# A third PSUM bank for transposed scores, shared with the value sums

## The chip, the cores and the metric

The kernel runs on one NeuronCore of one Trainium2 chip. The metric is device time in microseconds (us), from start to end of one execution. A NeuronCore has five engines that run their own instruction queues side by side: TensorE (PE in the profile; its weight loads are shown apart as PEld), VectorE (DVE), ScalarE (ACT), GpSimd (POOL) and SyncE (SP), which here issues the DMAs. TensorE writes its results to PSUM, which has 8 banks of 128 partitions x 512 fp32 values. GpSimd is used here on SBUF alone.

## The reference

With x of shape (1, 2048, 512), 32 heads of width 16, and a bilinear GLU of width 1792:

```
xn = layernorm(x)
q, k, v = split(xn @ wqkv)                       # 32 heads, 16 wide
p  = softmax(q @ k^T / 4)                        # per head, 2048 x 2048
s  = (p @ v) @ wo
g  = silu(((xn @ w_gate) * (xn @ w_up)) @ w_down)
out = x + s * g
```

## The kernel before

**Precision.** Projections and the GLU use matmuls of type fp32r, each operand split into a high and a low part and three products summed. GpSimd does most of the splitting (a cast and a subtraction, through the helper at L64, which therefore stands as the line of all GpSimd work).

**Attention units.** The work of attention is cut into 32 units: unit `i` is a group of four heads (`g = i // 4`) with one block of 512 queries (`c = i % 4`). A unit has 16 rounds, one for each tile of 128 keys; round `n` of the main loop (L832) is key tile `kt = n % 16` of unit `i = n // 16`. There are 512 rounds.

**One round.** For each of four heads `j`, `expo` (L600) makes a tile `t` of transposed scores (128 keys x 512 queries) on TensorE, in a PSUM bank with the tag "st", and ScalarE writes its exponential `e` to an SBUF tile (L606). `score` (L574) makes a tile `s` of untransposed scores for a unit that comes 21 tiles later, in a bank with the tag "s", and VectorE reduces it to a row maximum `mx` (L581); these maxima enter the transposed scores as extra contraction rows. `t` and `s` use opposite halves of the array's rows and run at the same time, so TensorE does them as pairs. In three of the four places of a round (GAPS) it also takes a few pairs of "filler" matmuls: the q and k projections (tile `p`, L270 and L274), then the GLU (tiles `g`, `u`, `y`), then the output projection (`z`). 93 filler sums share 240 pairs of rounds (CYCLES); most sums have 24 pairs of matmuls and get two or three pairs of rounds each.

**Value sums.** At the end of every even round, `values` (L820) issues the value matmuls of the two rounds before: `pv` (L609) does four matmuls for each key tile, one per head, each on its own 32 columns of the array; they are fp32 and take two passes, so 16 records stand for one block of two key tiles. All 16 key tiles of a unit accumulate in one PSUM bank of the tag "pv". From here on, a *period* means the two rounds from the end of one value block to the end of the next: eight pairs of `t` and `s` with filler pairs between them, and then the value block. There are 256 value blocks.

**After a unit.** `finish` (L618) is a generator that is stepped once per round. Its first step, right behind the unit's last value block, transposes the bank to SBUF on VectorE (`tr`, L623). The next round's step takes the reciprocal `rc` of the row sums (L626) and multiplies on GpSimd (`on`); the step five rounds later transposes back (L632) and stores to DRAM.

**Banks and buffers.** In the main loop BUFS (L43) shares the 8 banks out: 2 for `t`, 3 for `s`, 1 for `pv`, 2 ("misc") for filler. The tiles `e` have 12 buffers (EBUFS). When a value block is issued, 8 of them hold the two rounds it reads and 4 the round just made.

**Order.** TensorE, ScalarE and VectorE run in the order of the program (L828). GpSimd and SyncE are ordered by the scheduler of the framework, by when it finds an instruction ready. A queue runs in order whatever its head waits for.

Some of the small ScalarE and VectorE work has a fixed place in the round: the GLU's `g` copy (L375) and the product `h` (L377) stand at the end of an even round, around the value block; the copy `hh` (L335) stands one round later; `look` (L278) is a one-element read that makes the second half of a filler sum wait for the first.

Of the kernel before, what the change touches and what calls it, by code (L numbers as in the profile page):

```python
# [11 lines left out]
F32 = mybir.dt.float32  # L12
F32R = mybir.dt.float32r
AF = mybir.ActivationFunctionType
OP = mybir.AluOpType
# [4 lines left out]
P = 128  # L20
S, D, H, DH, FF = 2048, 512, 32, 16, 1792
NT = S // P
# [6 lines left out]
VW = DH + 1  # L29
# [10 lines left out]
FINAL_AT = 8  # L40
EARLY = [66, 75, 84, 93] + [104 + 37 * n // 4 for n in range(17)]
EARLY_BUFS = {"s": 4, "x": 2, "f": 2}
BUFS = {"st": 2, "s": 3, "pv": 1, "misc": 2}  # L43
LOWER, UPPER = slice(0, 64), slice(64, P)
BEHIND = mybir.DependencyInfo(mybir.DependencyClass.Sync, mybir.DependencyReason.DATA)
ORDER = mybir.DependencyInfo(mybir.DependencyClass.NoSync, mybir.DependencyReason.SCHED_ONLY)
# [3 lines left out]
def body(ctx, tc, x, wqkv, wo, wg, wu, wd, out):  # L50
# [66 lines left out]
    def psum(tag, name):  # L117
        ps, bufs = fst["ps"]
        return ps.tile([P, 512], F32, tag=tag, name=name, bufs=bufs[tag])
# [23 lines left out]
    def etile():  # L143
        return ep.tile([P, 512], F32, name="e", bufs=EBUFS)
# [395 lines left out]

    NU = NG * NC
    QS, MX = {}, {}

    def two(ap, e):

# [60 lines left out]
        nc.scalar.activation(e, o, AF.Exp, scale=DH ** -0.5)  # L606
        return e

    def pv(i, kt, es):  # L609
        g = i // NC  # L610
        if kt == 0:
            fst["pv"] = psum("pv", f"pv{i}")
        for j in range(4):
            h0 = (4 * g + j) * VW
            nc.tensor.matmul(fst["pv"][32 * j:32 * j + 32], V[:, kt, h0:h0 + 32], es[j],  # L615
                             start=kt == 0, stop=kt == NT - 1)

    def finish(i):  # L618

        g, c = divmod(i, NC)  # L620
        tr = keep.tile([P, 16, 32], F32, name="tr", bufs=1)
        tn = tr.rearrange("p b e -> p (b e)")
        nc.vector.transpose(tn, fst["pv"])  # L623
        yield
        rc = keep.tile([P, 16, 1], F32, name="rc", bufs=1)
        nc.vector.reciprocal(rc, tr[:, :, DH:DH + 1])  # L626
        late = i >= NU - NC
        (nc.vector if late else pool).tensor_tensor(on[:, :, 0:DH], tr[:, :, 0:DH], rc.to_broadcast([P, 16, DH]),
                                                         op=OP.mult)
        for _ in range(1 if late else 5):  # L630
            yield
        nc.vector.transpose(tn, on.rearrange("p b e -> p (b e)"))  # L632
        if i == NU - 1:
            fst["tn"] = tn
            return
        dma(OD[c][4 * g:4 * g + 4], tn)
        finished.add(i)
# [8 lines left out]
    def early():  # L646

        nc.scalar.activation(look, ones[0:1, 0:1], AF.Sqrt)
        for tt in range(4):
            load_x(tt)  # L650
        wraw = []
        for which in (1, 0):
            wraw.append(wtile(f"w{which}r"))
            dma(wraw[-1], wqkv[:, which * D:which * D + P].rearrange("(d p) f -> p d f", p=P))
        norm["raws"] = raws = [etile() for _ in range(ND)]
        for d in range(ND):
            dma(raws[d], wqkv[d * P:(d + 1) * P, 2 * D:])
        for tt in range(4, NT):
            load_x(tt)

        def ahead(m):
            fst["qk", m] = qk_weights(m, 1), qk_weights(m, 0)

        def exp_table(_):
            nc.scalar.activation(look, ones[0:1, 0:1], AF.Exp)

        def warm(n):
            for _ in range(n):
                nc.tensor.matmul(psum("x", "warm"), ident, on.rearrange("p b e -> p (b e)"), start=True, stop=True)

        warm(6)
        first = (0, 1), (2, 3)
        for tts in first:
            ln_open(tts)
        ln_stats(0)
        ln_stats(1)
        ln_root(first[0])
        ln_scale(first[0])
        ln_apply(0)
        ln_apply(1)  # L680
        ln_stats(2)
        ln_stats(3)
        ln_turn(0)
        ln_turn(1)
        warm(3)
        ln_root(first[1])
        ln_scale(first[1])
        ln_apply(2)
        last = ln_apply(3)
        ln_low(0)  # L690
        ln_low(1)
        ln_turn(3)
        ln_turn(2)
        ln_low(3)
        ln_low(2)
        wk, wq = [split_raw(f"w{which}", raw, last) for which, raw in zip((1, 0), wraw)]
        wv = [[etile().bitcast(F32R) for _ in range(ND)] for _ in range(2)]
        for d in range(ND):
            nc.scalar.activation(wv[0][d], raws[d], AF.Copy)
            pool.tensor_tensor(wv[1][d], raws[d], wv[0][d], op=OP.subtract)  # L700

        def k(c):
            yield from qk_proj(wk, 0, 1, c, "f")
            load_k(0, [c])

        def q(c):
            yield from qk_proj(wq, 0, 0, c, "f" if c else "x")
            load_q(c)

        def v(*tts):  # L710
            for tt in tts:
                yield from v_proj(wv, tt, "f")

        at = {n: [] for n in range(253)}
        for c, stats, apply, turns in ((1, (0, 2, 4, 6), (26, 26, 26, 26), (38, 42, 46, 50)),
                                       (2, (16, 20, 26, 27), (60, 60, 62, 62), (70, 74, 79, 83)),
                                       (3, (30, 34, 36, 38), (73, 73, 85, 85), (100, 106, 112, 118))):
            for t in range(4):
                for n, fn in ((stats[t], ln_stats), (apply[t], ln_apply), (turns[t], ln_turn)):
                    at[n].append((fn, 4 * c + t))  # L720
        for tts, n, root, scale in ((tuple(range(4, 8)), 0, 13, 25), (tuple(range(8, NT)), 16, 52, 53)):
            at[n].insert(0, (ln_open, tts))
            at[root].append((ln_root, tts))
            at[scale].insert(0, (ln_scale, tts))
        at[190].append((ones_rows, ks[0]))
        at[150].append((exp_table, None))
        at[205].append((ahead, 1))
        at[130] += [(ones_columns, slice(8, NT)), (other_keys, None)]
        fst["v"] = v_proj(wv, NT - 1, "pv")
        gens = [k(0), q(0), v(0, 1, 2), k(1), q(1), v(3), k(2), v(4, 5), k(3), v(*range(6, NT - 1))]  # L730
        scored = 0
        stream = (n for g in gens for n in g)
        for n in range(253):
            for fn, arg in at[n]:
                fn(arg)
            if n in EARLY:
                for _ in range(4):
                    r, j = divmod(scored, 4)
                    score(r // 16, r % 16, j)
                    scored += 1  # L740
                if scored == 64:
                    maxima(0, 0)
            next(stream, None)
        assert scored == 4 * LEAD
        return wq
# [25 lines left out]
    def step_small(q):  # L771
        if q and next(q[0], 1):
            q.pop(0)
# [44 lines left out]
    prev = []  # L818

    def values():  # L820
        for p in prev:
            pv(*p)
            if p[1] == NT - 1:
                heads.append(finish(p[0]))
                step_small(heads)
        prev.clear()

    with tc.manual_schedule(engines=ORDERED):  # L828
        with banks_of(EARLY_BUFS):
            fil = Filler(filler(early()), spread)  # L830
        ctx.enter_context(banks_of(BUFS))
        for n in range(NU * 16):  # L832
            now[0] = n
            Tied.on = n < 18
            i, kt = divmod(n, 16)
            g, c = divmod(i, NC)
            si, sr = divmod(n + LEAD, 16)
            if kt == 8 and i + 2 < NU:
                load_q(i + 2)
            if kt == 0 and g + 1 < NG and c == 1:  # L840
                load_k(g + 1)
            es = []
            for j in range(4):
                es.append(expo(i, kt, j))
                if si < NU:
                    score(si, sr, j ^ 1)
                step()
                if j == 1:
                    prepare()
                if n and j in GAPS[n % 2]:  # L850
                    if fil.done:
                        fil = Filler(ending(), lambda n: 2)
                    fil.part(n % 2 and j == 1)
            if sr == 15 and si < NU:
                maxima(si, 8 if si < NU - 1 else 4)
            step_small(heads)
            if kt % 4 == 2:
                soon(2, lambda: step_small(later))
            if n == 0:
                run(fst["v"])  # L860
            elif n % 2 == 0 or n == NU * 16 - 1:
                values()
            prev.append((i, kt, es))
        pv(*prev[0])
        run(finish(NU - 1))
        flush()
        last_heads()
        while fil.left or not fil.done:
            now[0] += 1
            prepare()  # L870
            fil.part()
            flush()
# [17 lines left out]
```

## Time and profile before

| | us |
|---|---|
| median of 3 runs | 1857.36 (1857.04 to 1858.09) |
| the profiled execution, its own time | 1857.28 |
| its span from first to last instruction | 1855.5 |
| TensorE matmul busy | 1825.2 |
| VectorE busy | 1474.1 |
| ScalarE busy | 1268.8 |
| GpSimd busy | 574.4 |

A row of a wait reads: who waited, for whom, then the total of that wait in us, how many times, and the longest. A row of the chain of work (which is followed back from the last instruction) reads: start, length, engine, tile and line. A row of the timeline reads: start, length, engine, line, operation and tiles, with the idle time before it and what ended it in brackets; x7 means seven instructions merged. A row of the groups has, after the count, busy time in us and the mean of one instruction in ns. Matmuls are pipelined and their ends are modelled, so a busy TensorE is not one at its peak.

### The profile page before, as it was taken

Reading aid. Unit: us, or ns where it says so; the run is one execution under the profiler, and the core shown is the slowest. Engines: PE = TensorE matmul, PEld = TensorE weight load, DVE = VectorE, ACT = ScalarE, POOL = GpSimd, SP = SyncE. Lnnn points to the kernel's source line nnn. Section 1 sums busy time; section 2 is a strip of 40 time slices with the busy share of each in tenths; the row PEclk is TensorE's granted clock in tenths of the full one; section 3 lists DMA queues with packets and bytes.
Section 4 is the critical chain, followed back from the end, with each engine's and each line's share of the span. In section 5 each row is a group of like instructions: output and inputs, shape, how many; then the busy total and the mean of one; then the engine's idle time right before and its main releaser. Section 6 shows DMA issues by size and latency. Waiting matters only on the chain.

```text
span 1855.5 us, 34207 instructions
## 1 busy us (share of the span) xinstructions
PE 1825.2 (98%) x13578; PEld 976.1 (53%) x13578; DVE 1474.1 (79%) x2438; ACT 1268.8 (68%) x2377; POOL 574.4 (31%) x641
## 2 busy tenths in 40 slices
PE   9999999999999999999999999999999999999998
PEld 5655555555455545555555554555545455454554
DVE  6878888888888888888888888888887888888832
ACT  6256767777766767767677777776767777667664
POOL 5312332532322333233132531421335233134340
PEclk9999999999999999999999999999999999999999
DMA  5317533511131212411023210411134111012341
GB/s 197 113 49 229 181 110 115 137 49 44 50 67 50 91 45 66 73 56 44 28 68 102 77 52 22 100 50 38 42 95 112 33 56 50 19 50 64 115 133 69
DMA packets 117227, 145.72 MB, mean 79 GB/s; under 512 B 12620, under 2 KB 74060, under 8 KB 114380
## 3 DMA queue, kind: packets, MB, share of 16 engines
q1 hardware_dynamic: 117068, 143.55, 26.5%
q8 instruction: 106, 1.74, 0.4%
q14 instruction: 53, 0.43, 0.1%
HBM read 95.94 MB, written 47.45 MB: 77 GB/s over the span
## 4 chain that ended last, share of the span: by engine, by line
PE 92%; ACT 6%; DVE 1%; issue 1%; POOL 0%; DMA 0%; ACTq 0%; POOLq 0%; DVEq 0%
PE pv L615 26%; PE t L604 25%; PE s L579 9%; PE u L270 5%; PE y L270 5%; PE g L270 4%; ACT e L606 4%; PE g L274 3%; PE u L274 3%; PE y L274 3%; PE v L251 2%; PE p L274 2%; PE z L270 2%; PE p L270 2%; ACT hh L335 1%; PE p L251 1%
## 5 line engine op out<-in xcount | busy, mean ns | idle before, releaser
L581 DVE TENSOR_REDUCE mx<-s 128x1 f32<-128x512 f32 x2048 | 1314.0, 684 | 279.9 <-PE s L579 176.5
L606 ACT ACTIVATE e<-t 128x512 f32<-128x512 f32 x2048 | 1161.5, 597 | 510.2 <-PE s L579 262.1
L604 PE MATMUL t<-qs,ks 50*128 50x512 f32 x2048 | 850.0, 436 | 18.3 <-ACT e L606 16.2
L579 PE MATMUL s<-ks,qs 48*128 48x512 f32 x2048 | 831.6, 436 | 0.8 <-DVE mx L581 0.8
L604 PEld LDWEIGHTS t<-qs,ks 50*128 50x128 f32 x2048 | 357.0, 184 | 510.4 <-ACT e L606 330.0
L615 PE MATMUL pv<-e,V 128*32 128x512 f32 x4096 | 493.8, 600 | 0.0
L579 PEld LDWEIGHTS s<-ks,qs 48*128 48x128 f32 x2048 | 349.1, 184 | 22.0 <-issue 5.0
L615 PEld LDWEIGHTS pv<-e,V 128*32 128x32 f32 x4096 | 107.1, 109 | 235.0 <-issue 226.5
L64 POOL CAST w0h<-w0r 128x512 fp32r<-128x512 f32 x60 | 36.7, 612 | 419.3 <-PE u L270 201.1
L64 POOL CAST dh<-wdr 128x512 fp32r<-128x512 f32 x56 | 33.7, 614 | 203.5 <-PE y L274 157.5
L64 POOL TENSOR_TENSOR hl<-h,hh 128x512 fp32r<-128x512 f32 x56 | 72.2, 1290 | 76.8 <-ACT hh L335 74.1
L274 PE MATMUL u<-fh,w0l 64*128 64x512 f32 x224 | 88.0, 393 | 0.0
L274 PE MATMUL u<-fl,w0h 64*128 64x512 f32 x224 | 87.9, 392 | 0.0
L270 PE MATMUL y<-dh,hh 64*128 64x512 f32 x224 | 87.9, 392 | 0.0
L270 PE MATMUL u<-fh,w0h 64*128 64x512 f32 x224 | 87.9, 392 | 0.0
L270 PE MATMUL g<-fh,w1l 64*128 64x512 f32 x224 | 87.8, 392 | 0.0
L270 PE MATMUL y<-dl,hh 64*128 64x512 f32 x224 | 87.8, 392 | 0.0
L274 PE MATMUL g<-fh,w1l 64*128 64x512 f32 x224 | 87.8, 392 | 0.0
L270 PE MATMUL y<-dh,hl 64*128 64x512 f32 x224 | 87.8, 392 | 0.0
L270 PE MATMUL u<-fh,w0l 64*128 64x512 f32 x224 | 87.7, 392 | 0.0
L274 PE MATMUL y<-dh,hh 64*128 64x512 f32 x224 | 87.7, 391 | 0.0
L274 PE MATMUL y<-dl,hh 64*128 64x512 f32 x224 | 87.7, 391 | 0.0
(253 smaller groups left out, 2902.5 us busy)
## 6 DMA issues: line engine op xcount, KB each, us to landing
w1r<-in_wg_dram SPq DMA_DIRECT2D x56, 256.0 KB
w0r<-in_wu_dram SPq DMA_DIRECT2D x56, 256.0 KB
wdr<-in_wd_dram SPq DMA_DIRECT2D x56, 256.0 KB
qs<-QD SPq DMA_DIRECT2D x64, 192.0 KB
ks<-KD SPq DMA_DIRECT2D x12, 768.0 KB
KD<-hl SPq DMA_DIRECT2D x16, 512.0 KB
QD<-hl SPq DMA_DIRECT2D x16, 512.0 KB
OD<-tr SPq DMA_DIRECT2D x31, 256.0 KB
```

The source lines that it names most:

```text
L64: got = getattr(self.engine, name)(*args, **kw)
L251: nc.tensor.matmul(o, l(d), r(d), start=k == d == 0, stop=k == 2 and d == ND - 1)
L270: nc.tensor.matmul(outs[k], l[LOWER], r[LOWER], start=k == 0 and n == 0, stop=(stop or k == 0) and n == len(low) - 1, skip_group_check=k == 1)
L274: nc.tensor.matmul(outs[1 - k], l[UPPER], r[UPPER], start=k == 0 and m == 0, stop=(stop or k == 0) and m == len(high) - 1, skip_group_chec ...
L335: nc.scalar.activation(hi, h, AF.Copy)
L579: nc.tensor.matmul(o, QS[i][b:b + KB, pr, t * P:(t + 1) * P], k[b:b + KB, pr, kc * 512:(kc + 1) * 512], start=True, stop=True)
L581: nc.vector.tensor_reduce(MX[i][:, j, t, kc:kc + 1], o, axis=AX.X, op=OP.max)
L604: nc.tensor.matmul(o, k[b:b + KR, pr, kt * P:(kt + 1) * P], QS[i][b:b + KR, pr], start=True, stop=True)
L606: nc.scalar.activation(e, o, AF.Exp, scale=DH ** -0.5)
L615: nc.tensor.matmul(fst["pv"][32 * j:32 * j + 32], V[:, kt, h0:h0 + 32], es[j], start=kt == 0, stop=kt == NT - 1)
```

## The change

The bank of the tag "pv" is given to "st", which then has three. A value block takes its bank from the "st" banks in turn, like a tile of scores, so that in a period nine tiles pass through three banks. The value sums of a unit are now kept in an SBUF tile (`acc`, one buffer) and each block of two key tiles is added to it: the first block of a unit is copied there by ScalarE; the six in the middle are copied by ScalarE to a tile from the `e` buffers, which GpSimd adds to the sum; the last one is added by VectorE, straight from PSUM (in the very last unit its last two key tiles are two blocks of one, both added by VectorE). `finish` begins with an empty step, and then transposes from `acc` instead of from PSUM.

```diff
-BUFS = {"st": 2, "s": 3, "pv": 1, "misc": 2}
+BUFS = {"st": 3, "s": 3, "misc": 2}
...
+    sums = {}
...
-    def pv(i, kt, es):
+    def block(todo):
+
+        i = todo[0][0]
         g = i // NC
-        if kt == 0:
-            fst["pv"] = psum("pv", f"pv{i}")
-        for j in range(4):
-            h0 = (4 * g + j) * VW
-            nc.tensor.matmul(fst["pv"][32 * j:32 * j + 32], V[:, kt, h0:h0 + 32], es[j],
-                             start=kt == 0, stop=kt == NT - 1)
+        o = psum("st", f"pv{i}")
+        for n, (_, kt, es) in enumerate(todo):
+            for j in range(4):
+                h0 = (4 * g + j) * VW
+                nc.tensor.matmul(o[32 * j:32 * j + 32], V[:, kt, h0:h0 + 32], es[j],
+                                 start=n == 0, stop=n == len(todo) - 1)
+        if todo[0][1] == 0:
+            sums[i] = keep.tile([P, 512], F32, name="acc", bufs=1)
+            nc.scalar.activation(sums[i], o, AF.Copy)
+        elif kt >= NT - 2:
+            nc.vector.tensor_tensor(sums[i], o, sums[i], op=OP.add)
+        else:
+            part = etile()
+            nc.scalar.activation(part, o, AF.Copy)
+            pool.tensor_tensor(sums[i], sums[i], part, op=OP.add)
 
     def finish(i):
 
...
         tn = tr.rearrange("p b e -> p (b e)")
-        nc.vector.transpose(tn, fst["pv"])
+        yield
+        nc.vector.transpose(tn, sums.pop(i))
         yield
...
-        fst["v"] = v_proj(wv, NT - 1, "pv")
+        fst["v"] = v_proj(wv, NT - 1, "st")
...
     def values():
-        for p in prev:
-            pv(*p)
-            if p[1] == NT - 1:
-                heads.append(finish(p[0]))
-                step_small(heads)
+        block(prev)
+        if prev[-1][1] == NT - 1:
+            heads.append(finish(prev[0][0]))
+            step_small(heads)
         prev.clear()
...
-        pv(*prev[0])
+        block(prev)
         run(finish(NU - 1))
```

## The prediction

> **What bounds the kernel now.** I read the page first (span, busy times, chain), then the waits, then the chain and the timeline of single periods.
>
> ```profile
> span 1855.5 us, 34207 instructions
> PE 1825.2 (98%) x13578; PEld 976.1 (53%) x13578; DVE 1474.1 (79%) x2438; ACT 1268.8 (68%) x2377; POOL 574.4 (31%) x641
> PE 92%; ACT 6%; DVE 1%; issue 1%; POOL 0%; DMA 0%; ACTq 0%; POOLq 0%; DVEq 0%
> ```
>
> TensorE looks full: 98% busy and 92% of the chain, so 30.3 us of its time seems free. The waits say otherwise:
>
> ```profile
> PEld t L604 <- ACT e L606: 330.0, 839, 1.0
> ACT e L606 <- PE s L579: 262.1, 168, 1.7
> POOL w0h L64 <- PE u L270: 201.1, 19, 13.1
> POOL w0h L64 <- PE g L274: 164.1, 29, 7.7
> PEld s L579 <- DVE mx L581: 4.4, 10, 0.9
> ```
>
> The weight load of `t` waits 839 times for an exponential, which must free the bank. The bank of `s` makes TensorE wait 4.4 us in all. What one wait costs is seen in a period. First the chain of one with twelve filler pairs:
>
> ```profile
> 206.58 1.85 PE pv L615 x16
> 208.43 0.42 PE t L604
> 208.85 0.23 PE s L579 x2
> ...
> 209.57 0.47 PE t L604
> ...
> 213.57 1.85 PE pv L615 x16
> ```
>
> Each pair takes 0.23 (0.233 over many), the value block 1.85, the first `t` behind it 0.42. Only the third `t` takes 0.47. The timeline shows why:
>
> ```profile
> 208.89 4.61 ACT L606 ACTIVATE e<-t 128x512 f32<-128x512 f32 x7 [1.40 <-PE s L579]
> 208.93 5.39 DVE L581 TENSOR_REDUCE mx<-s 128x1 f32<-128x512 f32 x8 [0.97 <-PE s L579]
> 209.54 0.18 PEld L604 LDWEIGHTS t<-qs,ks 50*128 50x128 f32 x1 [0.41 <-ACT e L606]
> 209.54 0.50 PE L604 MATMUL t<-qs,ks 50*128 50x512 f32 x1
> ```
>
> With two banks the third `t` needs the bank of the first. That exponential starts at 208.89 and takes 0.60; the load follows at 209.54 and the matmul ends at 210.04. So a `t` ends no earlier than 0.55 after its bank is freed. Both ScalarE and VectorE start a period late, after idling through the value block (1.40 and 0.97). Now a period with eight filler pairs:
>
> ```profile
> 303.03 0.42 PE t L604
> ...
> 307.70 1.85 PE pv L615 x16
> ```
>
> Without waits, a period with f filler pairs takes 0.42 + 7 x 0.233 + 0.233 f + 1.85 = 3.90 + 0.233 f.
>
> - Twelve pairs: 6.70, against 213.57 + 1.85 - 208.43 = 6.99.
> - Eight pairs: 5.77, against 307.70 + 1.85 - 303.03 = 6.52: with fewer filler pairs between them, more than one `t` waits.
>
> ```profile
> 112.72 1.85 PE pv L615 x16
> ...
> 1838.86 1.95 PE pv L615 x16
> ```
>
> Between the first and the last value block lie 255 periods of 6.77 on average. Counted in the timeline, 116 hold eleven or twelve filler pairs (some 6.99 each); the other 139 then average (255 x 6.77 - 116 x 6.99) / 139 = 6.59.
>
> **The change part by part.** Prices of one instruction come from these groups:
>
> ```profile
> L581 DVE TENSOR_REDUCE mx<-s 128x1 f32<-128x512 f32 x2048 | 1314.0, 684 | 279.9 <-PE s L579 176.5 <-PE t L604 93.0
> L606 ACT ACTIVATE e<-t 128x512 f32<-128x512 f32 x2048 | 1161.5, 597 | 510.2 <-PE s L579 262.1 <-PE t L604 147.7
> L375 ACT ACTIVATE g<-g 128x512 f32<-128x512 f32 x56 | 33.2, 593 | 0.0
> L632 DVE STREAM_TRANSPOSE tr<-on 128x512 f32<-128x512 f32 x32 | 22.4, 701 | 0.1
> L402 DVE TENSOR_TENSOR y<-y,y 128x512 f32<-128x512 f32 x32 | 21.6, 675 | 0.0
> L64 POOL TENSOR_TENSOR y<-e,y 128x512 f32<-128x512 f32 x16 | 20.6, 1286 | 1.2
> ```
>
> *The third bank and the copy.* Nine tiles pass through three banks in each period, so the third `t` behind a value block always gets the block's own bank, and waits for its copy. The copy has the form of L375: 0.59. It starts as soon as the block ends, for ScalarE idles there. Taking the end of the block as zero, it runs from 0.05 to 0.65 and lets the third `t` end at 0.65 + 0.55 = 1.20. TensorE reaches that point by itself at 0.42 + 4 x 0.233 = 1.35, so the wait is gone with 0.15 to spare. Each later `t` needs the exponential of the one three before. These come every 0.50 to 0.60, from 0.55 on; the fourth `t` may end at 1.15 + 0.55 = 1.70, and TensorE is there at 2.05 with two filler pairs between. Twelve pairs: nothing waits for ScalarE, saving 6.99 - 6.70 = 0.29, times 116 = 34 us.
>
> *What is late next in short periods.* `s` has three banks and VectorE. In the eight-pair period VectorE starts 0.50 after the block:
>
> ```profile
> 303.53 4.36 DVE L581 TENSOR_REDUCE mx<-s 128x1 f32<-128x512 f32 x7 [1.21 <-PE s L579]
> ```
>
> Seven in 4.36 with a last one of 0.68 is one every 0.61. The last `s` needs the fifth reduction, which starts at 0.50 + 4 x 0.61 = 2.94 and ends at 3.62: the `s` can't end before 4.17, while TensorE would be there at 0.42 + 15 x 0.233 = 3.92. So VectorE sets 4.17 + 1.85 = 6.02. I take 6.11 over the 139, since seven- and nine-pair periods and the extra ScalarE copies (`g`, `hh`) land unevenly. Saved: 6.59 - 6.11 = 0.48, times 139 = 67 us. Bounds: the nearest rows allow 0.80 (TensorE alone, 5.79) and 0.2 (only the third `t` mended).
>
> *ScalarE's load.* 32 x 7 = 224 copies of 0.59 are 133 us, giving 1402 of a span near 1790. They run where ScalarE idled (262.1 us behind value blocks). `hh` in the same period pushes an exponential by 0.6; I charge 0.1 for each of 56, 6 us. If the idle time were gone, all 133 would count.
>
> *VectorE.* The 33 adds of 0.68 stand where the first transposition stood, waiting for the same block: no net change. But the empty first step moves the first transposition (L623) one round on, from the value block's shadow to the middle of a period, and the one back (L632, 0.70) with it, from an even to an odd round; I price both at 0.70. In a short period VectorE has no slack, so each costs 0.70; in a twelve-pair one its slack is 4.85 - 4.17 = 0.68, and it costs nothing. 62 x 139/255 x 0.70 = 24 us. The reciprocal (0.23) moves the other way: 3 us back. Bounds: 0 if the idle time behind the block absorbs them, 43 if none is.
>
> *GpSimd.* 192 sums of 1.29 are 248 us, on an engine busy 574 of 1855. Who waits for a sum? In a period without the change 8 buffers `e` are free after a block and 8 are taken before the next. The copied block is a ninth, so the last exponential of the period takes the buffer of that copy, and waits for GpSimd. The sum can start at 0.65 and end at 1.94; the exponential is only missed when it holds up the next copy, at 6.02 - 0.60 = 5.4. Slack 3.4. Nearly everything queued on GpSimd fits:
>
> ```profile
> 591.21 0.61 POOL L64 CAST w0h<-w0r 128x512 fp32r<-128x512 f32 x1 [9.89 <-PE u L270]
> ...
> 593.58 1.29 POOL L64 TENSOR_TENSOR w1l<-w1r,w1h 128x512 fp32r<-128x512 f32 x1
> ```
>
> This run of four splits lasts 3.7. The larger run, at the twelve starts of a third of the GLU, does not:
>
> ```profile
> 572.29 1.17 POOL L64 CAST dh<-wdr 128x512 fp32r<-128x512 f32 x2 [27.54 <-PE y L274]
> ...
> 580.04 1.28 POOL L64 TENSOR_TENSOR dl<-wdr,dh 128x512 fp32r<-128x512 f32 x1
> ```
>
> From 572.29 to 581.32, 9.0 us; a sum behind all of it is 5.6 late. Bounds 0 and 12 x 5.6 = 67; I take 6, since the scheduler orders GpSimd by what is ready, so that a sum can go between two splits.
>
> *Nothing else.* The value matmuls stay the same in number; DMAs keep their number and sizes (stores and the loads behind them move one round). At the end of the kernel one add of 0.68 joins the serial tail: 1 us.
>
> **Sum.** -34 - 67 + 6 + 24 - 3 + 6 + 1 = -67 against the profiled execution's 1857.28 (span 1855.5, and 1.8 around it; the median of the runs is 1857.36, the same within 0.01%). 1857 - 67 = 1790.
>
> **Rivals.**
>
> *Sums come late (slower).* GpSimd's queue is in order, and its casts wait in it for TensorE: `w0h` for (201.1 + 164.1) / 48 = 7.6 on average. A sum behind such a cast holds the period's last exponential 7.6 - 3.4 = 4.2 too long, and TensorE with it. The gain is used up at 67 / 4.2 = 16 of the 60 casts `w0h`; 20 of them give 1874, half of them 1916. Against it: a cast is freed by a matmul that TensorE reaches in fixed order just before a value block, while the sum is ready just after. The Trainium skill's page "PSUM — Partial Sum Buffer", section "Engine vs sequencer instructions", calls the GpSimd queue strict FIFO; the bracketed 9.89 us wait above agrees.
>
> *VectorE binds in all short periods.* The moved transpositions, `h` and the maxima no longer fit behind the shorter period, and only half of the short periods' gain stays: 1790 + 34 = 1824. For it: VectorE would be busy over 80% with three banks of slack; against it, 0.97 to 1.21 idle behind every block.
>
> *The slack absorbs all.* Neither the moved transpositions nor the sums cost anything: 1857 - 101 + 7 = 1763.
>
> *The change does not do what it says.* The value block's bank is freed too late (a copy held up over 0.15), so the third `t` waits as before: 1850 to 1857. By busy time the room would be 30.3 and the result 1827 at best. The Trainium skill's "Perfetto Trace Analysis", section "Identifying the Most-Contended Engine", says that matmul busy time does not measure headroom and that the same gap repeating can mean too little PSUM; the 0.47 in every period agrees.
>
> **How the numbers follow.** Forecast 0.45 (own range 1775 to 1808), late sums 0.15, VectorE 0.20, all absorbed 0.15, no effect 0.05. The range runs from 1752 to 1860, leaving out most of the late sums and a little below the absorbed case. A measurement of this kernel tells a change from none at about 0.2%, 3.7 us. Faster: 0.45 + 0.20 + 0.15 = 0.80; same 0.05; slower 0.15.
>
> **What would show it.** Right: waits of `t` for `e` fall from 330 us to under 120; the third `t` of a period takes 0.23; twelve-pair periods last 6.7; waits of `s` for `mx` grow from 4.4 us to some tens, in periods with a transposition above all; ScalarE busy near 1400, GpSimd near 820. Wrong: rows in which `e` or VectorE's add waits for GpSimd with totals over 60 us, or the copy starting more than 0.2 after its block.

## The result

The changed kernel takes 1807.41 us (median of four runs, 1804.11 to 1810.13) beside 1857.20 before: a ratio of 0.9731 (95% interval 0.9714 to 0.9748), 50 us faster. The forecast was 1790, with a range of 1752 to 1860.

The page of the profiled execution (1807.26 us):

```profile
span 1805.0 us, 35056 instructions
PE 1767.9 (98%) x13578; PEld 1056.4 (59%) x13578; DVE 1455.0 (81%) x2471; ACT 1323.7 (73%) x2601; POOL 821.8 (46%) x833
PE 86%; DVE 4%; POOL 3%; ACT 2%; DMA 2%; issue 1%; SPq 0%; POOLq 0%; DVEq 0%; ACTq 0%
```

TensorE's busy share is 98%, as before. What moved is the share of weight loads (53% to 59%), and the chain: VectorE, GpSimd and even a DMA now stand in it.

The waits:

```profile
PEld t L605 <- ACT e L607: 107.8, 268, 6.0
PEld s L580 <- DVE mx L582: 23.4, 46, 2.5
ACT e L607 <- POOL acc L64: 22.4, 9, 6.8
PEld t L605 <- ACT e L627: 13.6, 49, 0.7
```

`t` waited 839 times before and waits 268 times now. Three waits are new or larger: `s` for the maxima, an exponential for a GpSimd sum, and `t` for the copy of a value block (L627, which writes a tile of the `e` buffers). The last is small, 13.6 us in all.

The chain through a period with twelve filler pairs, and through one with eight:

```profile
211.18 0.42 PE t L605
...
212.31 0.24 PE t L605
...
216.13 1.85 PE pv L618 x16
217.99 0.43 PE t L605
```

```profile
198.45 0.43 PE t L605
...
199.57 0.23 PE t L605
...
202.58 1.85 PE pv L618 x16
204.44 0.42 PE t L605
```

The third `t` takes 0.24 and 0.23 where it took 0.47. The eight-pair period lasts 204.44 - 198.45 = 5.99, against 6.52 before and 6.02 in the forecast. This twelve-pair period lasts 6.81, because it is the one behind a unit's last block; the median of those not there is 6.73, against 6.99 before and 6.70 in the forecast. So these two periods do what was foretold, and the time that is missing lies elsewhere.

### The profile page after: what moved, and what is told of

Same layout as the page of the kernel before. It is cut to its first block, busy times and chain, and to the rows that moved or that the text cites. A ratio compares the mean times of both kernels' runs of the same rounds, so it can differ in the third digit from the quotient of the medians.

```text
span 1805.0 us, 35056 instructions
## 1 busy us (share of the span) xinstructions
PE 1767.9 (98%) x13578; PEld 1056.4 (59%) x13578; DVE 1455.0 (81%) x2471; ACT 1323.7 (73%) x2601; POOL 821.8 (46%) x833
## 4 chain that ended last, share of the span: by engine, by line
PE 86%; DVE 4%; POOL 3%; ACT 2%; DMA 2%; issue 1%; SPq 0%; POOLq 0%; DVEq 0%; ACTq 0%
PE pv L618 25%; PE t L605 17%; PE s L580 12%; PE g L270 5%; PE u L270 4%; PE y L270 4%; PE y L274 4%; PE u L274 3%; PE g L274 3%; DVE mx L582 3%; PE p L270 3%; PE v L251 2%; PE z L270 1%; ACT e L607 1%; PE p L274 1%
## 5 line engine op out<-in xcount | busy, mean ns | idle before, releaser
L582 DVE TENSOR_REDUCE mx<-s 128x1 f32<-128x512 f32 x2048 | 1276.8, 681 | 247.3 <-PE s L580 163.2
L607 ACT ACTIVATE e<-t 128x512 f32<-128x512 f32 x2048 | 1110.8, 609 | 126.4 <-PE t L605 32.2
L605 PE MATMUL t<-qs,ks 50*128 50x512 f32 x2048 | 805.8, 415 | 15.8 <-ACT e L607 14.3
L64 POOL TENSOR_TENSOR acc<-acc,e 128x512 f32<-128x512 f32 x192 | 251.0, 1307 | 455.8 <-ACT e L627 455.8
L627 ACT ACTIVATE e<-pv 128x512 f32<-128x512 f32 x192 | 114.7, 598 | 221.6 <-PE pv L618 221.6
L274 PE MATMUL g<-fh,w1h 64*128 64x512 f32 x224 | 90.7, 405 | 0.0
L270 PE MATMUL u<-fh,w0h 64*128 64x512 f32 x224 | 89.1, 398 | 0.0
L274 PE MATMUL u<-fh,w0h 64*128 64x512 f32 x224 | 88.8, 396 | 0.0
L274 PE MATMUL u<-fh,w0l 64*128 64x512 f32 x224 | 88.5, 395 | 0.0
L270 PE MATMUL g<-fh,w1l 64*128 64x512 f32 x224 | 88.4, 395 | 0.0
L270 PE MATMUL g<-fl,w1h 64*128 64x512 f32 x224 | 88.3, 394 | 0.0
L270 PE MATMUL g<-fh,w1h 64*128 64x512 f32 x224 | 88.2, 394 | 0.0
```

What stands on the lines that cost most here:

```text
L64: got = getattr(self.engine, name)(*args, **kw)
L270: nc.tensor.matmul(outs[k], l[LOWER], r[LOWER], start=k == 0 and n == 0, stop=(stop or k == 0) and n == len(low) - 1, skip_group_check=k == 1)
L274: nc.tensor.matmul(outs[1 - k], l[UPPER], r[UPPER], start=k == 0 and m == 0, stop=(stop or k == 0) and m == len(high) - 1, skip_group_chec ...
L582: nc.vector.tensor_reduce(MX[i][:, j, t, kc:kc + 1], o, axis=AX.X, op=OP.max)
L605: nc.tensor.matmul(o, k[b:b + KR, pr, kt * P:(kt + 1) * P], QS[i][b:b + KR, pr], start=True, stop=True)
L627: nc.scalar.activation(part, o, AF.Copy)
```

## The experiments

All times are medians of four runs, with the kernel before timed on the same chip.

### Sums in SBUF without the third bank

```diff
-BUFS = {"st": 3, "s": 3, "misc": 2}
+BUFS = {"st": 2, "s": 3, "pv": 1, "misc": 2}
...
-        o = psum("st", f"pv{i}")
+        o = psum("pv", f"pv{i}")
...
-        fst["v"] = v_proj(wv, NT - 1, "st")
+        fst["v"] = v_proj(wv, NT - 1, "pv")
```

> The sums in SBUF as in the changed kernel, but the value block keeps a bank of its own and the transposed scores have two. Theory (the third bank is the gain, and copies and sums alone cost): the copy stands ahead of the first exponential, so the third t of a period waits 0.5 us longer in 224 periods and more than one t waits in short ones: 1930 to 1980, waits of t for e over 400 us. Rival (the gain comes from the value sums leaving PSUM, not from the bank): 1800 to 1815.

Measured: 1907.52 us, ratio 1.0274 (1.0257 to 1.0291).

```profile
PEld t L605 <- ACT e L607: 354.7, 833, 4.9
```

```profile
208.06 1.90 PE pv L618 x16
209.96 0.02 issue
209.98 0.60 ACT e L627
210.58 0.50 ACT e L607
211.08 0.04 issue
211.12 0.49 PE t L605
...
215.13 1.86 PE pv L618 x16
216.99 0.42 PE t L605
```

The waits of `t` are back (833), and the kernel is slower than before. With and without the bank differ by 1907.5 - 1807.4 = 100 us: that is what the bank gives once the sums are in SBUF. The sums alone cost 1907.5 - 1856.5 = 51 us beside the kernel before. The rival is refuted: taking the value sums out of PSUM gains nothing by itself.

The expected time was too high. The chain shows the error: copy (0.60) and exponential (0.50 behind it) end 1.12 after the block, where the first exponential alone ended 1.06 after it in the period shown of before (209.49 - 208.43). ScalarE had to wait some 0.46 for its first `t` anyway, and the copy fills that time. It costs the twelve-pair periods 0.1 in the median (7.09 against 6.98; 7.03 against 6.99 in the ones shown), not 0.5.

### The third bank from the maxima

The kernel before, with one number moved:

```diff
-BUFS = {"st": 2, "s": 3, "pv": 1, "misc": 2}
+BUFS = {"st": 3, "s": 2, "pv": 1, "misc": 2}
```

> The kernel before with the third bank for t taken from s (two left), value sums in PSUM as before. Theory (VectorE is the next limit): the wait of t goes, that of s for the maxima takes its place; twelve-pair periods about 6.75 to 6.9, short ones 6.5 to 6.7, in all 1830 to 1860, waits of s for mx over 150 us. Rival (three banks of s are not needed): 1755 to 1775, better than the changed kernel, since no copies or sums are added.

Measured: 1903.43 us, ratio 1.025 (1.0235 to 1.0265).

```profile
PEld s L579 <- DVE mx L581: 140.7, 441, 2.5
PEld t L604 <- ACT e L606: 38.8, 50, 0.9
```

The wait of `t` falls from 330 to 38.8 us, and that of `s` rises from 4.4 to 140.7, near what was expected of the waits. But the time lies 43 us above the top of what was expected: even twelve-pair periods grow, to a median of 7.09, and short ones last 6.9 whether they hold seven, eight or nine filler pairs. The third bank helps only if it isn't one of VectorE's.

### Late sums taken over by VectorE

In the trace of the changed kernel, 12 of the 192 GpSimd sums end so late that the last exponential of the period starts 0.03 us behind them. The worst case follows: the timeline of GpSimd, that of ScalarE, and then busy times by stretch. A row of the last has the stretch, its length, the busy times of PE, PEld, DVE, ACT and POOL with their instructions, the granted clock (1.00 is full speed), the DMA share and GB/s.

```profile
337.07 0.61 POOL L64 CAST dh<-wdr 128x512 fp32r<-128x512 f32 x1 [3.76 <-DMA wdr<-in_wd_dram]
...
339.54 1.26 POOL L64 TENSOR_TENSOR acc<-acc,e 128x512 f32<-128x512 f32 x1
```

```profile
340.83 0.60 ACT L607 ACTIVATE e<-t 128x512 f32<-128x512 f32 x1 [6.75 <-POOL acc L64]
```

```profile
335.00:341.40 6.40, 0.84 (x6) 0.19 (x2) 1.09 (x2) 0.57 (x2) 4.25 (x5) 0.81 0.41 101
341.40:346.00 4.60, 4.52 (x22) 3.54 (x24) 2.47 (x4) 3.22 (x7) 4.52 (x6) 0.52 0.42 112
346.00:350.00 4.00, 4.00 (x38) 1.90 (x34) 2.89 (x5) 2.43 (x5) 4.00 (x4) 1.00 0.44 128
```

A split of `dh` at the head of GpSimd's queue waits for its weights; the sum stands behind it; the exponential needs the buffer of the copy; the next value block's copy stands behind that exponential. TensorE stops. The period lasts 14.60 (335.41 to 350.01) instead of 6.73, 7.9 more. The stop is 5.6 of that; the rest comes after it, where the clock is at 0.52 and matmul pairs take 0.43. Here ten of the eleven blocks whose sum ended more than 4 us behind its copy are added by VectorE instead (the eleventh held up nothing):

```diff
+LATE = {1, 11, 21, 33, 34, 84, 188, 235, 241, 243}
...
-        elif kt >= NT - 2:
+        elif kt >= NT - 2 or 8 * i + todo[0][1] // 2 in LATE:
             nc.vector.tensor_tensor(sums[i], o, sums[i], op=OP.add)
```

> The changed kernel, but the ten value blocks whose GpSimd sum ended more than 4 us after its copy are added by VectorE straight from PSUM, like the last block of a unit. Theory (the rest of the missing gain is exponentials that wait for a late sum, because its copy holds one of the 12 buffers, and the slower TensorE clock behind such a stop): waits of e for GpSimd fall from 22 us to under 8, the stops of 8 us near 335 us and of 5 us near 1650 us go, and the time falls by 8 to 16 us, to 1791 to 1799. Rival (the added work costs, not its lateness: 182 of 192 sums and all copies but ten stay): 1804 to 1808.

Measured: 1793.98 us, ratio 0.9665 (0.965 to 0.9679), 13 us less than the changed kernel. The same place:

```profile
327.00:342.00 15.00, 15.00 (x124) 8.72 (x124) 13.20 (x22) 10.24 (x22) 9.22 (x10) 1.00 0.67 146
```

TensorE is busy all through at full clock, although 182 sums and copies are still there. So these 13 us are the price of lateness, not of the amount of work. One of the stops that should have gone stays: near 1640 us the filler `y` waits 1.8 us for GpSimd to split its operand (`hl`), and that period lasts 9.35 where it lasted 6.54 before. In the kernel before no filler waits for GpSimd. So late work on GpSimd reaches TensorE in a second way, which the prediction did not have.

### Where the transpositions stand

Two edits of the first step of `finish`. One takes the empty step out; the other, shown here, makes it two, except in the last four units, which get none.

```diff
-        yield
+        for _ in range(0 if i >= NU - NC else 2):
+            yield
         nc.vector.transpose(tn, sums.pop(i))
```

> The changed kernel without the empty step of finish, so the first transposition stands right behind VectorE's add at the end of the value block, and the second is back in an even round. Theory: the second transposition (8 us) and the end (7 us) are won back, but add and transposition now hold the first reduction of the next period by 0.7 us in all 32 units, also those with twelve filler pairs, 10 to 15 us: 1799 to 1808. Rival (the empty step is the whole fault): 1778 to 1786.

> The changed kernel, but finish makes two empty steps in units 0 to 27, which puts both transpositions at the end of an even round, and none in units 28 to 31, which end as early as in the kernel before. Theory (a transposition costs where it stands in the middle of a short period, some 20 us in all; the empty step in the last units leaves a hole without filler, some 7 us): 1778 to 1786, short periods behind a unit's last block 6.0 to 6.3 instead of 6.8, and 15 us instead of 22 behind the last value block. Rival (VectorE has no idle time left, so 0.7 us costs the same wherever it stands): only the end is gained, 1799 to 1803.

Measured: without the empty step 1800.79 us, ratio 0.97 (0.9686 to 0.9715); with two 1785.37 us, ratio 0.9622 (0.9606 to 0.9638). Both times fit the theory and refute the rivals; only the stretch behind the last value block fell less than expected, to 19 us. The chain of the changed kernel through a period with eight filler pairs behind a unit's last block, and that of the kernel with two empty steps:

```profile
263.87 0.66 PE t L605 x2
...
266.42 0.67 DVE mx L582
267.08 0.62 DVE tr L636
267.70 0.59 DVE mx L582
...
268.83 1.85 PE pv L618 x16
270.69 0.66 PE t L605 x2
```

```profile
263.52 0.66 PE t L605 x2
...
267.53 0.24 PE t L605
267.89 1.85 PE pv L618 x16
269.74 0.43 PE t L605
```

With the transposition between two reductions, the last `s` of the period waits for VectorE and the period lasts 6.82. With the transposition at the end of an even round, where VectorE idles through a value block, it lasts 6.22. Without any empty step add and transposition both stand behind the block: every period behind a unit's last block is longer, those with twelve pairs too (7.35 against 6.73), which takes most of the gain back. (Of the 22 us of two empty steps, some 3 come from the end of the kernel, not from the periods.)

### VectorE adds every block

```diff
-        elif kt >= NT - 2:
+        elif True:
             nc.vector.tensor_tensor(sums[i], o, sums[i], op=OP.add)
```

> The changed kernel with all seven later blocks of a unit added by VectorE straight from PSUM; no ScalarE copies but the first of a unit, no GpSimd sums. Theory (VectorE binds short periods and has slack in long ones): each add holds the first reduction of the next period by some 0.2 us and the row of reductions behind it by 0.7; the short periods go from 6.0 to 6.2 up by 0.2 to 0.6, the twelve-pair ones by less than 0.1, the 16 us of late sums go: 1825 to 1865. Rival (VectorE's idle time behind a value block hides the add, as it hid the first transposition): 1785 to 1800.

Measured: 1804.60 us, ratio 0.9717 (0.9703 to 0.9732): the same as the changed kernel, without GpSimd sums and with one ScalarE copy a unit.

```profile
L624 DVE TENSOR_TENSOR acc<-pv,acc 128x512 f32<-128x512 f32 x225 | 155.2, 690 | 168.9 <-PE pv L618 166.7
```

The expected time was too high. The add (0.69) begins at once behind the block, so the first reduction starts only some 0.2 later. The median eight-pair period goes from 5.99 to 6.15, the twelve-pair one stays at 6.73. What the short periods lose, the late sums give back.

### Repairs together

Two empty steps (none in the last four units) and the ten late blocks on VectorE (called late_two below); the same with every block from the 233rd on, and the 156th, on VectorE too; and two empty steps with every block on VectorE.

> Both repairs together: two empty steps in finish (none in units 28 to 31), and the ten late blocks added by VectorE. Theory (two separate faults, transpositions in the middle of a period and late sums): the gains add, 1807 - 22 - 13 = 1772, within 1768 to 1776. Rival (both win back the same lost time, or VectorE's ten adds collide with the transpositions now at the end of even rounds): 1779 to 1785.

> As late_two, with every block from the 233rd on (unit 29 and after, where GpSimd splits the operands of the output projection and VectorE has few maxima left) added by VectorE, and the 156th too. Theory (late sums stop TensorE there and nothing else does): 2 to 6 us below late_two. Rival (the stops of the last units come from GpSimd's splits themselves, or from the hole without filler): the same as late_two within 2 us.

> All seven later blocks of a unit added by VectorE, and the two empty steps of finish (none in units 28 to 31). Theory (what an add costs VectorE behind a block, 0.2 us in a short period, does not grow when a transposition stands ahead of that block): 1804 - 22 = 1782, within 1778 to 1788, slower than late_two, because every short period still pays for its add. Rival (the row of reductions, the transposition and the add together overfill the time of the value block): 1792 to 1804.

| kernel | us | ratio (95%) |
|---|---|---|
| two empty steps, ten blocks on VectorE | 1773.38 | 0.9551 (0.9533 to 0.9568) |
| the same kernel again, on the chip of the last row | 1774.10 | 0.9558 (0.9542 to 0.9574) |
| and all blocks at the end | 1774.26 | 0.9555 (0.954 to 0.9569) |
| two empty steps, all blocks on VectorE | 1790.82 | 0.9641 (0.9626 to 0.9655) |

> The same kernel as late_two, beside all_dve_two on one chip: 1771 to 1777.

The two gains add (1807 - 22 - 13 = 1772): they are separate faults. The first of these kernels is the fastest found, 84 us faster than before. More blocks on VectorE at the end win nothing. With all blocks on VectorE, two empty steps give 14 instead of 22 us, less than the theory and a little more than the rival expected; the median of the twelve-pair periods right behind the second transposition is 6.98 instead of 6.73, which fits transposition and add meeting at one value block, but no run takes that apart.

## Why the prediction was right, and what it missed

The same period holds the same TensorE work in every kernel, so the traces can be subtracted period by period. The two kinds of period are taken from the kernel before and late_two, which has neither late sums of more than 6 us nor, in units 0 to 27, transpositions in the middle of a period; what little both still cost there counts against the bank. The other terms are differences between late_two, the kernel with the late blocks on VectorE alone, the changed kernel and the kernel before.

| term of the sum | forecast | measured |
|---|---|---|
| third bank and copies, long periods (eleven or twelve pairs) | -34 | -31 |
| third bank and copies, short periods, with `hh` | -67 + 6 = -61 | -55 |
| transpositions and reciprocal, in the periods | 24 - 3 = 21 | 14 |
| late sums | 6 | 14 |
| start and end of the kernel | 1 | 8 |
| sum | -67 | -50 |

The sum is 17 us off, and only by luck not more: the transpositions cost 7 less than foretold, which hides some of what the other terms cost more. The 100 us between the kernels with and without the bank can't be set against the forecast's 34 + 67 = 101: the one is counted from a kernel that already has the sums and is 51 us slower, the other from the kernel before. From there bank and copies give 31 + 55 = 86, against 95. The trace has 121 long periods (6.96 on average before) and 134 short ones (6.60), not 116 and 139; this moves the sum by little.

*What bounds the kernel.* Right. A TensorE at 98% busy still had 84 us to give, and its busy share is 98% after the gain too. The wait of `t` for `e` is 107.8 us, under the 120 foretold.

*The third bank and the copy; what is late next in short periods.* Right for the two periods that were worked out: the medians of twelve- and eight-pair periods not behind a unit's last block are 6.73 and 5.99, against 6.70 and 6.02 in the forecast. VectorE does set the eight-pair ones. In the one shown, which begins at 198.45, the fifth reduction and the load of the last `s` are:

```profile
201.35 0.68 DVE L582 TENSOR_REDUCE mx<-s 128x1 f32<-128x512 f32 x1
202.09 0.18 PEld L580 LDWEIGHTS s<-ks,qs 48*128 48x128 f32 x1
```

The load follows the end of the reduction (202.03) by 0.06. In 21 of the 22 eight-pair periods that lie clear of the steps of `finish` it follows by less than 0.09; the rows of the waits hardly show this, since the weight loads idle so briefly. And the transposed period above is 0.6 longer for 0.7 more on VectorE.

What the forecast had wrong is the seven-pair periods, 48 of the 134 short ones. They last 6.22, longer than eight-pair ones. The forecast let two filler pairs stand ahead of the third `t`; here it is one, so TensorE is there at 0.42 + 3 x 0.233 = 1.12, 0.08 ahead of the 1.20 that the copy allows. In all 29 that lie clear of `finish` the third `t` is loaded within 0.09 of the end of the copy, and it takes 0.31 instead of 0.23 in the median; most of the next three `t` follow an exponential as closely. So ScalarE holds these periods as well as VectorE. Over all short periods late_two has 6.19 on average, where 6.11 was taken.

*ScalarE's load.* The forecast of 1400 us busy was too high: it is 1323.7. The copies take 114.7 + 19.2 us, but the busy time of the exponentials falls from 1161.5 to 1110.8, because they now stand in longer rows, in which one starts about 0.5 after the other and overlaps it (seven of 0.60 in 3.60, from 199.01, in the eight-pair period shown).

*VectorE.* Right in mechanism: the empty step was the cost, at the places named, and the twelve-pair periods all but hid it (medians 6.73 and 6.82). The size was put too high, 21 us for 14: a short period grows by less than the 0.70 that was charged for each.

*GpSimd.* This is the term that was most undersized, 6 us for 14. The chain of causes was as told: the copied block is a ninth buffer, the last exponential of a period waits for the sum. But the price of 6 us came from the twelve starts of a third of the GLU alone and left out what follows a stop. One such start held up an exponential for 6.8 us; others stood among the splits for the output projection, and some in the first 260 us. And the longest stop of TensorE, 5.6 us, was followed by a stretch at half clock, which added some 2 us. Together the ten late blocks cost 13 us by the medians. The rival of late sums named the right waiter but the wrong reason: in the worst case shown the cast ahead of the sum waited for a DMA, not for TensorE.

*The end.* It was charged 1 us and cost 7.4. Its chain, in the changed kernel:

```profile
1780.99 1.93 PE pv L618 x16
1782.92 0.02 issue
1782.94 0.70 DVE acc L624
```

Behind the last value block it needs 1805.0 - 1782.9 = 22.1 us, where the kernel before needs 1855.5 - 1840.8 = 14.7: the add of 0.70 that was charged, and filler of the output projection that is left over. Without the empty step it needs 15.7, and with two, but none in the last units, 19.0, though the last units run the same program in both. So the empty step is not all of it; the rest was not traced.

## What to carry to other kernels

Judge a full TensorE by what its weight loads wait for, and price one such wait in the chain of a single period; the sum over 255 periods came out at 95 us here, and 86 were measured. Price each kind of period by itself: the short periods that missed were the seven-pair ones, for which no period was worked out. When a result leaves PSUM by two engines, ask which buffer the intermediate copy takes and who needs it next: the sum was off the path in 180 cases of 192, and ten of the others cost 13 us. A step moved by one round of a loop can leave the shadow that hid it, even if nothing is added.

## What was not expected of the hardware

After TensorE had stopped for 5.6 us, its clock was granted at 0.52 for the next 4.6 us and matmul pairs took 0.43 instead of 0.23; then it was back at 1.00, as the three stretches of the late sum show. The Trainium skill's page "TensorE: Matmul & The Clock Gate", in "Part 1: The HAM clock gate (the "warmup" mystery)", states half rate after an idle window of about 3.4 us and full rate after a busy one as long; the stretches agree. The stretch without filler near the end of the changed kernel, where TensorE waits for copies between short runs of `t`, has a low clock too, 0.71:

```profile
1745.00:1762.00 17.00, 16.35 (x64) 5.46 (x58) 0.00 (x0) 10.72 (x21) 5.27 (x5) 0.71 0.04 13
```

There no gap of TensorE in the chain or the timeline is over 0.8 us, so here the clock was low without a stop of several us. What set it there was not tested.
